# One ScalarE Silu in place of Tanh and a VectorE multiply, with the exponentials run in a row, in a fused attention and feed-forward kernel

## Chip, cores, metric

The kernel runs on one core of one Trainium2 chip. The metric is device time in microseconds; a kernel's figure is the median of its runs. All runs told here were of the fast state. Where two kernels are compared by a ratio, it is the mean time of one kernel's fast runs over that of the other's fast runs of the same rounds on the same chip, so it is not quite the ratio of the medians quoted beside it. In the traces PE is TensorE, PEld its weight loads, DVE is VectorE, ACT is ScalarE, POOL is GpSimd, and SPq is the DMA queue that SyncE feeds. "Idle" of an engine is time in which it runs nothing; an arrow names what ended that idle.

## The reference, cut

```python
def _attn_ref(q, k, v):                       # q, k, v: (8, 8, 576, 64), fp32
    q_s = np.exp(q - max_d); q_s = q_s / sum_d(q_s)      # softmax over the head dimension
    k_s = np.exp(k - max_s); k_s = k_s / sum_s(k_s)      # softmax over the sequence
    kv  = np.einsum('bhsd,bhse->bhde', k_s, v)
    return np.einsum('bhsd,bhde->bhse', q_s, kv)

def _moe_ref(x, w_in, w_out):                 # x: (4608, 512), d_ff = 2048
    h = x @ w_in
    g = h * (1.0 / (1.0 + np.exp(-h)))        # SiLU
    return g @ w_out
# output = _moe_ref(attention output, heads side by side)
```

So there are eight batches of attention, which need exponentials, and 4608 rows of a feed-forward layer, which need SiLU.

## The kernel before

The rows are worked in nine chunks of 512 (the first two have 576 and 448). The first product of a chunk, called mm1, has 16 blocks. Each fills one bank (a tile of 128 x 512 fp32 values in PSUM, `hps`), and ScalarE and VectorE empty it into `GT`. The banks come from a ring of five, which the attention's small products share.

```python
    PSB = {"ring": 5, "ops": 3}
    ...
    def mm1(t, fb):
        for off, size in part[t]:
            hps = ps.tile([128, TCH], FP32, name="hps", tag="ring", bufs=PSB["ring"])
            for c in range(NC):
                nc.tensor.matmul(out=hps[:, 0:size], lhsT=W1[...], rhs=XT[t][...], ...)
            sg = mp.tile([128, TCH], FP32, name="sg", bufs=3)
            nc.scalar.activation(out=sg[:, 0:size], in_=hps[:, 0:size], func=ACT.Tanh, scale=0.5)
            ...
                nc.vector.scalar_tensor_tensor(        # (tanh(h/2) + 1) * h = 2 SiLU(h)
                    out=GT[g][:, fb, col:col + n], in0=sg[:, h], scalar=1.0,
                    in1=hps[:, h], op0=ALU.add, op1=ALU.mult)
```

The factor of 2 is taken back by a scale of 0.5 where results are copied out. The second product is plain (`mm2`) for chunks 0 and 1. From chunk 2 on it is a Strassen scheme of seven half-size products, each in two parts, which needs sums and differences of GT blocks, made on VectorE (`presum`, tiles `SW`). A chunk's second product trails behind the mm1s of the next chunk.

Attention of batch `b` is woven into the list of these products, which the kernel calls units. `begin[b]` is the unit of chunk `b`'s first mm1, and a plan says how many units earlier each step is put into the program:

```python
    def exp(b, src, dst, cc):                          # 1152 columns of one half (cc) of q or k
        ...
        nc.scalar.activation(out=o, in_=jgd(st[b][src], cc), func=ACT.Exp)

    def plan_attn(b, u, sm, vs, tp, ks, ox, eng=nc.gpsimd):
        for cc in range(2):
            plan(u + sm[cc], lambda cc=cc: exp(b, "qt", "eq", cc))
            plan(u + sm[cc] + 1, lambda cc=cc: (qsum(b, cc), qnorm(b, cc, nc.gpsimd)))
        for cc in range(2):
            plan(u + sm[2 + cc], lambda cc=cc: exp(b, "kt", "ek", cc))
            plan(u + vs[cc], lambda cc=cc: vcast(b, cc, eng))
        plan(u + tp, lambda: tr_dma(b, nc.sync))       # qT: transposed by DMA
        ...                                            # loads of batch b + 1
        for cc in range(2):
            plan(u + ks[cc], lambda cc=cc: kv(b, cc))  # key-value products, two ring banks
            ...
        for cc in range(2):
            plan(u + ox[cc], lambda cc=cc: xt(b, cc))  # attention output -> XT, input of mm1
    ...
    for b in range(4, B):
        plan_attn(b, begin[b], (-38, -34, -30, -26), (-32, -28), -19, (-14, -10), (-7, -4))
```

`qsum` sums on VectorE, and `qnorm` multiplies and `vcast` casts on GpSimd. In the timelines below ScalarE and VectorE run their work in the order in which the program issues it (ScalarE at 151.52, 152.59 and 153.76 us, for one); so what is planned earlier also stands in front of what is planned later.

The softmax here doesn't subtract the row's maximum and nothing guards it: scores larger than these inputs give would overflow.

## Time and profile before

| | before |
|---|---|
| median of 4 runs | 283.75 us (282.66 to 283.88) |
| span of the profiled execution | 280.2 us |
| busy: TensorE / VectorE / ScalarE | 266.2 / 211.0 / 151.8 us |
| TensorE idle | 14.0 us |

These are the head and three lines of the groups from the page of the kernel before. Group lines read: line, engine, operation, tiles, size and count, then total busy us and mean ns of one, then idle of the engine before them and what ended it. PEclk is the granted TensorE clock in forty slices, in tenths.

```profile
span 280.2 us, 5788 instructions
PE 266.2 (95%) x2306; PEld 162.6 (58%) x2306; DVE 211.0 (75%) x393; ACT 151.8 (54%) x250; POOL 57.0 (20%) x44
PEclk9999999999999999999999999999999999999998
...
L214 ACT ACTIVATE sg<-hps 128x512 f32<-128x512 f32 (+3 forms) x160 | 87.5, 555 | 91.4 <-PE hps L206 68.4
L222 DVE SCALAR_TENSOR_TENSOR GT<-sg,hps 128x512 bf16<-128x512 f32 (+2 forms) x176 | 97.6, 582 | 44.3 <-ACT sg L214 43.7
L91 ACT ACTIVATE eq<-qt 128x1152 bf16<-128x1152 f32 x16 | 18.6, 1169 | 3.1 <-DMA qt<-in_q_dram 3.1
```

TensorE is the bound: 95% busy at full clock. The table of stretches shows where its 5% of idle is. The columns are the length, then busy us and count for each engine, then clock.

```profile
core 0: us, PE busy (x) PEld busy (x) DVE busy (x) ACT busy (x) POOL busy (x), PEclk, DMA share, GB/s
...
80.00:100.00 20.00, 18.84 (x166) 8.50 (x165) 16.56 (x32) 15.32 (x25) 5.92 (x5) 1.00 0.81 260
100.00:120.00 20.00, 20.00 (x210) 13.13 (x209) 17.97 (x33) 10.89 (x18) 4.36 (x3) 1.00 0.70 222
120.00:140.00 20.00, 20.00 (x145) 12.83 (x146) 17.82 (x26) 13.14 (x21) 7.36 (x4) 1.00 0.56 143
```

Next, ScalarE at the turn of a chunk: single exponentials stand between other work, and the one table load of the program is at its start.

```profile
0.73 1.28 ACT L366 ACT_TABLE_LOAD   x1 [0.73 <-PEq L534]
2.03 0.20 ACT L366 ACTIVATE dummy<-dummy 1x1 f32<-1x1 f32 x1
...
151.52 1.18 ACT L91 ACTIVATE eq<-qt 128x1152 bf16<-128x1152 f32 x1
152.59 1.28 ACT L214 ACTIVATE sg<-hps 128x512 f32<-128x512 f32 x2
153.76 1.15 ACT L91 ACTIVATE ek<-kt 128x1152 bf16<-128x1152 f32 x1
```

The load took 1.28 us and the next activation began 0.02 us after it. Tanh and Exp alternate without a load.

### The profile page before, as it was taken

What the parts mean: (1) busy time and instruction counts of PE and PEld (TensorE: products, weight loads), DVE (VectorE), ACT (ScalarE), POOL (GpSimd) and SP (SyncE); (2) the same over time, 40 slices, a digit from 0 to 9 for tenths busy, and PEclk for the clock granted to TensorE, in tenths of its full rate; (3) what the DMA queues carried; (4) which work ended last, traced back from release to release, by engine and by line L of the source; (5) the groups of instructions that cost most, each with busy time, mean ns of one, the idle gap of its engine ahead of it and who ended that gap; (6) DMA issues with size and microseconds to landing.
All of it is one profiled execution on the core that took longest, in us unless ns stands there. A gap on an engine that the chain in (4) does not pass through costs nothing.

```text
span 280.2 us, 5788 instructions
## 1 busy us (share of the span) xinstructions
PE 266.2 (95%) x2306; PEld 162.6 (58%) x2306; DVE 211.0 (75%) x393; ACT 151.8 (54%) x250; POOL 57.0 (20%) x44
## 2 busy tenths in 40 slices
PE   8689989988999999999999999999999999999992
PEld 3366654434444366666666666666666665666882
DVE  3975656896669898879987998799858585767721
ACT  5664663862785875476548654865265444544100
POOL 1551140063170370037003700370000000000000
PEclk9999999999999999999999999999999999999998
DMA  7999999988539949532982398235122013110244
GB/s 259 288 195 272 309 294 220 390 297 199 229 72 346 322 81 336 219 74 58 282 331 60 74 290 320 63 75 65 40 66 49 0 37 77 37 32 8 57 95 112
DMA packets 42378, 46.44 MB, mean 166 GB/s; under 512 B 18544, under 2 KB 29808, under 8 KB 42352
## 3 DMA queue, kind: packets, MB, share of 16 engines
q1 hardware_dynamic: 37312, 38.35, 46.7%
q0 software_dynamic: 5040, 7.73, 12.4%
q8 instruction: 18, 0.29, 0.4%
q14 instruction: 8, 0.07, 0.1%
HBM read 36.70 MB, written 9.44 MB: 165 GB/s over the span
## 4 chain that ended last, share of the span: by engine, by line
PE 75%; DMA 11%; DVE 9%; POOL 2%; issue 1%; ACT 1%; SPq 0%; ACTq 0%; DVEq 0%
PE hps L206 36%; PE ops L282 31%; DMA W<-in_moe_w_out_dram 8%; PE ops L340 5%; DVE GT L222 3%; DMA vt<-in_v_dram 3%; PE kvps L153 2%; DVE TW L258 2%; PE o L187 2%; DVE zq L105 1%; POOL W L381 1%; POOL W L387 1%; DVE oq L353 0%; SPq L82 0%; DVE kvn L166 0%
## 5 line engine op out<-in xcount | busy, mean ns | idle before, releaser
L206 PE MATMUL hps<-XT,W 128*128 128x512 bf16 (+3 forms) x640 | 143.1, 358 | 1.2 <-DVE GT L222 0.5
L214 ACT ACTIVATE sg<-hps 128x512 f32<-128x512 f32 (+3 forms) x160 | 87.5, 555 | 91.4 <-PE hps L206 68.4
L222 DVE SCALAR_TENSOR_TENSOR GT<-sg,hps 128x512 bf16<-128x512 f32 (+2 forms) x176 | 97.6, 582 | 44.3 <-ACT sg L214 43.7
L206 PEld LDWEIGHTS <-W 128*128 128x128 bf16 x640 | 61.2, 98 | 49.9 <-issue 3.5
L111 POOL TENSOR_TENSOR eq<-eq,rzq 128x1152 bf16<-128x1152 bf16 x14 | 30.4, 2174 | 117.9 <-DVE rzq L106 59.7
L282 PEld LDWEIGHTS <-GT 128*128 128x128 bf16 x448 | 43.5, 98 | 14.9 <-issue 1.0
L282 PEld LDWEIGHTS <-SW 128*128 128x128 bf16 x336 | 32.9, 98 | 11.1
L340 PE MATMUL ops<-W,GT 128*128 128x512 bf16 x128 | 33.1, 380 | 3.4 <-DVE GT L222 2.4
L282 PE MATMUL ops<-W,GT 128*128 128x256 bf16 x224 | 28.7, 273 | 0.0
L282 PE MATMUL ops<-TW,SW 128*128 128x256 bf16 x224 | 28.7, 273 | 0.0
L282 PE MATMUL ops<-TW,GT 128*128 128x256 bf16 x224 | 28.6, 273 | 0.0
L105 DVE TENSOR_REDUCE zq<-eq 128x18 f32<-128x1152 bf16 x16 | 21.6, 1348 | 6.4 <-ACT eq L91 6.4
L198 ACT CAST XT<-o 128x512 bf16<-128x512 f32 (+3 forms) x36 | 18.4, 564 | 6.8 <-PE o L187 6.8
L340 PEld LDWEIGHTS <-GT 128*128 128x128 bf16 x128 | 11.9, 98 | 15.8 <-DVE GT L222 3.6
L91 ACT ACTIVATE eq<-qt 128x1152 bf16<-128x1152 f32 x16 | 18.6, 1169 | 3.1 <-DMA qt<-in_q_dram 3.1
L91 ACT ACTIVATE ek<-kt 128x1152 bf16<-128x1152 f32 x16 | 18.5, 1157 | 1.6 <-DMA kt<-in_k_dram 1.6
L98 POOL CAST vaug<-vt 128x1152 bf16<-128x1152 f32 x12 | 17.7, 1503 | 0.0
L282 PE MATMUL ops<-W,SW 128*128 128x256 bf16 x112 | 14.2, 273 | 0.0
L240 DVE TENSOR_TENSOR SW<-GT 128x1024 bf16<-128x1024 bf16 x14 | 13.2, 943 | 0.3
L244 DVE TENSOR_TENSOR GT<-GT 128x1024 bf16<-128x1024 bf16 x14 | 13.4, 956 | 0.0
L299 DVE SCALAR_TENSOR_TENSOR u<-ops,s 128x512 f32<-128x512 f32 x14 | 9.6, 683 | 4.6 <-PE ops L282 4.6
L299 DVE SCALAR_TENSOR_TENSOR oq<-ops,u 128x512 f32<-128x512 f32 x14 | 9.6, 684 | 2.1 <-PE ops L282 2.1
(44 smaller groups left out, 125.8 us busy)
## 6 DMA issues: line engine op xcount, KB each, us to landing
qt<-in_q_dram SPq DMA_DIRECT2D x6, 1152.0 KB, 6.4
kt<-in_k_dram SPq DMA_DIRECT2D x6, 1152.0 KB, 8.8
vt<-in_v_dram SPq DMA_DIRECT2D x6, 1152.0 KB, 11.2
out_dram<-oq SPq DMA_DIRECT2D x42, 128.0 KB, 2.4
out_dram<-oq SPq DMA_DIRECT2D x60, 64.0 KB, 2.0
W<-in_moe_w_in_dram POOLq DMA_DIRECT2D x4, 512.0 KB, 9.7
W<-in_moe_w_out_dram POOLq DMA_DIRECT2D x4, 512.0 KB, 17.8
qt<-in_q_dram SPq DMA_DIRECT2D x2, 576.0 KB, 4.2
```

Source lines behind the costliest of these rows:

```text
L91: nc.scalar.activation(out=o, in_=jgd(st[b][src], cc), func=ACT.Exp)
L98: eng.tensor_copy(o, jgd(st[b]["vt"], cc))
L105: nc.vector.reduce_sum(out=st[b]["zq"][:, cc], in_=e, axis=AX.X)
L111: eng.tensor_tensor(out=e, in0=e, in1=r[:, :, :, None].to_broadcast([128, J, 2, D]), op=ALU.mult)
L198: nc.scalar.copy(out=x, in_=o1[g][:, 0:size])
L206: nc.tensor.matmul(out=hps[:, 0:size], lhsT=W1[:, c, fb * 128:(fb + 1) * 128], rhs=XT[t][:, c, off:off + size], start=(c == 0), stop=(c == ...
L214: nc.scalar.activation(out=sg[:, 0:size], in_=hps[:, 0:size], func=ACT.Tanh, scale=0.5)
L222: nc.vector.scalar_tensor_tensor(out=GT[g][:, fb, col:col + n], in0=sg[:, h], scalar=1.0, in1=hps[:, h], op0=ALU.add, op1=ALU.mult,)
L244: V.tensor_sub(quad(t, 0, f, 1), quad(t, 0, f, 0), quad(t, 0, f, 1))
L282: nc.tensor.matmul(out=o[:, a, :], lhsT=l(f), rhs=r(f), start=bool(first and a == 0 and f == 0), stop=(f == HF - 1), skip_group_check=True,)
L299: nc.vector.scalar_tensor_tensor(out=out, in0=o, scalar=0.5, in1=x, op0=ALU.mult, op1=ALU.add)
L340: nc.tensor.matmul(out=OP[t, tb], lhsT=GT[t][:, fc, tb * 128:(tb + 1) * 128], rhs=W2[:, fc, :], start=(fc == 0), stop=(fc == NFB - 1),)
```

## The change

The intent is to take 97.6 us of multiplies off VectorE by letting ScalarE write the finished SiLU. The built program shows the price: Silu and Exp need different tables, so ScalarE has to load a table at each change between them. To keep these few, exponentials are put in a row: two and two for batches 1 to 3, all four for batches 4 to 7. The program has 22 table loads in place of 1.

```diff
-            sg = mp.tile([128, TCH], FP32, name="sg", bufs=3)
-            nc.scalar.activation(out=sg[:, 0:size], in_=hps[:, 0:size], func=ACT.Tanh, scale=0.5)
...
-                nc.vector.scalar_tensor_tensor(
-                    out=GT[g][:, fb, col:col + n],
-                    in0=sg[:, h], scalar=1.0, in1=hps[:, h], op0=ALU.add, op1=ALU.mult,
-                )
+                nc.scalar.activation(out=GT[g][:, fb, col:col + n], in_=hps[:, h], func=ACT.Silu)
... (the five scales of 0.5 behind the second product become 1.0)
-        for cc in range(2):
-            plan(u + sm[cc], lambda cc=cc: exp(b, "qt", "eq", cc))
-            plan(u + sm[cc] + 1, lambda cc=cc: (qsum(b, cc), qnorm(b, cc, nc.gpsimd)))
+        for i, (x, y) in enumerate((("qt", "eq"), ("kt", "ek"))):
+            plan(u + sm[i], lambda x=x, y=y: [exp(b, x, y, cc) for cc in range(2)])
         for cc in range(2):
-            plan(u + sm[2 + cc], lambda cc=cc: exp(b, "kt", "ek", cc))
+            plan(u + sm[0] + 2 + 2 * cc, lambda cc=cc: (qsum(b, cc), qnorm(b, cc, nc.gpsimd)))
             plan(u + vs[cc], lambda cc=cc: vcast(b, cc, eng))
...
-    plan_attn(1, begin[1], (-18, -17, -11, -10), (-6, -5), -12, (-4, -3), (-2, 0), V)
-    plan_attn(2, begin[2], (-23, -21, -18, -15), (-14, -13), -15, (-10, -7), (-5, -3))
-    plan_attn(3, begin[3], (-26, -24, -20, -17), (-19, -16), -16, (-12, -9), (-6, -4))
+    plan_attn(1, begin[1], (-18, -11), (-6, -5), -11, (-4, -3), (-2, 0), V)
+    plan_attn(2, begin[2], (-21, -18), (-14, -13), -13, (-10, -7), (-5, -3))
+    plan_attn(3, begin[3], (-25, -20), (-19, -16), -16, (-12, -9), (-6, -4))
     for b in range(4, B):
-        plan_attn(b, begin[b], (-38, -34, -30, -26), (-32, -28), -19, (-14, -10), (-7, -4))
+        plan_attn(b, begin[b], (-34, -34), (-32, -28), -23, (-14, -10), (-7, -4))
```

More of the change, by code (lines that the diff above doesn't have):

```diff
@@ L221, in mm1 @@
                 h = slice(a - first, a - first + n)
-                nc.vector.scalar_tensor_tensor(
-                    out=GT[g][:, fb, col:col + n],
-                    in0=sg[:, h],
-                    scalar=1.0,
-                    in1=hps[:, h],
-                    op0=ALU.add,
-                    op1=ALU.mult,
-                )
+                nc.scalar.activation(out=GT[g][:, fb, col:col + n], in_=hps[:, h], func=ACT.Silu)
                 a += n
@@ L299, in add @@
             nc.vector.scalar_tensor_tensor(
-                out=out, in0=o, scalar=0.5, in1=x, op0=ALU.mult, op1=ALU.add
+                out=out, in0=o, scalar=1.0, in1=x, op0=ALU.mult, op1=ALU.add
             )
         if k == 1:
-            nc.scalar.activation(out=new("s1"), in_=o, func=ACT.Copy, scale=0.5)
+            nc.scalar.activation(out=new("s1"), in_=o, func=ACT.Copy, scale=1.0)
         elif k == 6:
@@ L311, in after @@
             if k == 2:
-                nc.scalar.activation(out=q, in_=o, func=ACT.Copy, scale=0.5)
+                nc.scalar.activation(out=q, in_=o, func=ACT.Copy, scale=1.0)
             else:
@@ L352, in store @@
         if dve:
-            nc.vector.tensor_scalar_mul(out=ost, in0=OP[t, tb], scalar1=0.5)
+            nc.vector.tensor_scalar_mul(out=ost, in0=OP[t, tb], scalar1=1.0)
         else:
-            nc.scalar.activation(out=ost, in_=OP[t, tb], func=ACT.Copy, scale=0.5)
+            nc.scalar.activation(out=ost, in_=OP[t, tb], func=ACT.Copy, scale=1.0)
         for i in range(2):
```

## The prediction

> **What bounds the kernel now.** TensorE. The page gives PE 266.2 of 280.2 us busy; in the stage table it is 20.00 of every 20 us from 100 to 260. It idles 14 us in all: about 4 before 20 us, 1.0 near 38 (a weight load), 3.8 between 40 and 100 (nearly all released by the VectorE multiply into GT), 5 at the end. VectorE (211 us) and ScalarE (152 us) are off the critical path after 100 us. So a free SiLU could gain only about 4 us.
>
> **Removed.** 176 VectorE multiplies, 97.6 us (678 ns for 512 columns): VectorE falls to about 113 us.
>
> **Added, on ScalarE.** Silu should cost what Tanh costs (597 ns; one can start every 0.49 us). The Trainium skill, "ScalarE: Activation LUTs", "The pipeline for one element", says all functions run at one element per cycle; no run here shows Silu yet. Silu and Exp do not share a table: the built program has 21 further table loads (4 each for batches 1 to 3, 2 each for 4 to 7, one at the start). The one in the trace takes 1283 ns, with 0.02 us until the next activation. The same page, "What ACT_TABLE_LOAD costs", gives about 2.66 us with a drain; I count 1.28. 21 x 1.28 = 27 us: ScalarE rises to about 180 us, still not full. The sum is not the cost.
>
> **Moved, on the critical path: the bursts.** Exponentials start every 1.07 us. Two with their switches block ScalarE for 4.8 us, four for 6.9, and no hps bank is emptied meanwhile. The ring has 5 banks; PE fills one in 0.87 us where mm1s come in a row. And the first Strassen product of a chunk needs the GT of that chunk's mm1 number 14, now queued behind the burst. Laid over the old timeline:
> - Batches 5 to 7: burst right after the XT copies. At 150 us: copies end 151.6, load 152.9, exponentials 157.3, load 158.6, Silu 159.2. PE wants that GT at 157.4: 1.85 us of stall each, 5.5 us.
> - Batch 4: mm1s without products between; five banks full at 98.9, freed at 102.7: 3.8 us, less 0.9 of old stalls: +2.9.
> - Batch 3: an XT copy behind a burst: 2.4 us, partly in place of old stalls: +1.5.
> - Batch 2: two bursts with one Silu between, 10 us; mm2 stalls 4.2 us against 2.4: +1.8.
> - Batch 1: two ring stalls of 0.8 to 0.9, partly hidden by the weight wait: +0.9.
>
> Sum +12.6 us.
>
> **Prediction.** 296.5 us (+4.5%), 8 in 10 between 289 and 304. Faster by over 2%: 0.02; within 2%: 0.10; slower by over 2%: 0.88.
>
> **What would show each step.** Table loads: 22 of about 1.28 us. Silu near 597 ns. DVE near 113 us, ACT near 180. PE busy hardly changed, but idle of 1.5 to 4 us at each burst, released by ScalarE's Silu (GT) or XT copy; none in the last two chunks, which have no exponentials. The chain of waits should pass through ACT there.
>
> **What would make it wrong.** Loads that cost a drain as well: each burst 2.8 us longer, some 20 us in all. Silu slower than Tanh. Bursts that fall where PE has slack, so that most stalls vanish: then within 2%. Long stalls could also lower the granted clock, which the PEclk slices would show. If late key loads hold up the exponentials, ScalarE would wait for DMA inside the burst.

## More of the kernel before

The kernel before took 281.7 to 286.0 us over all its runs, on several chips, so a difference of 1 us between calls means nothing by itself; waits read from traces are sharper.

From 100 us on nothing is left to gain on TensorE but the last few microseconds. The idle that VectorE's multiply makes lies before that, at three places. The timeline of TensorE shows the longest (idle before an instruction, and what ended it, stands in brackets):

```profile
64.27 0.39 PE L340 MATMUL ops<-W,GT 128*128 128x512 bf16 x1 [2.13 <-DVE GT L222]
```

After 20 us there are five idles of TensorE in that timeline: 0.96 (a weight load), 0.26, 2.13, 0.38 and 0.52 us, 4.25 us in all.

## The result, and the profile after

| | before | after |
|---|---|---|
| median | 283.75 us | 304.62 us (303.96 to 305.71, 4 runs) |
| ratio | 1 | 1.075, 95% interval 1.070 to 1.079 |
| span of the profiled execution | 280.2 us | 303.3 us |
| TensorE busy / idle | 266.2 / 14.0 us | 272.2 / 31.1 us |
| VectorE busy | 211.0 us | 121.0 us |
| ScalarE busy | 151.8 us | 178.7 us |

The page of the changed kernel, the lines that answer to those above:

```profile
span 303.3 us, 5523 instructions
PE 272.2 (90%) x2306; PEld 163.3 (54%) x2306; DVE 121.0 (40%) x217; ACT 178.7 (59%) x287; POOL 53.9 (18%) x44
PEclk9999999997999968999999999999999999999999
...
L220 ACT ACTIVATE GT<-hps 128x512 bf16<-128x512 f32 (+2 forms) x176 | 85.5, 526 | 86.9 <-PE hps L206 86.4
L220 ACT ACT_TABLE_LOAD x11 | 14.1, 1283 | 0.2
```

Silu of 512 columns took 602 ns (Tanh: 597), and each load 1283 ns. ScalarE is 59% busy, so it is not short of time in sum. TensorE lost 17.1 us to idle, and its busy time grew by 6.0 us at the same work. The timeline of TensorE names the idles; one of each kind for batches 5 to 7 is kept here:

```profile
36.05 1.14 PE L206 MATMUL hps<-XT,W 128*128 128x320 bf16 x8 [1.70 <-ACT GT L220]
43.00 1.14 PE L206 MATMUL hps<-XT,W 128*128 128x320 bf16 x8 [1.27 <-ACT GT L220]
67.68 0.39 PE L331 MATMUL ops<-W,GT 128*128 128x512 bf16 x1 [4.28 <-ACT GT L220]
83.27 2.21 PE L206 MATMUL hps<-XT,W 128*128 128x512 bf16 x8 [1.98 <-ACT GT L220]
90.73 1.89 PE L206 MATMUL hps<-XT,W 128*128 128x512 bf16 x8 [0.94 <-ACT GT L220]
110.06 3.57 PE L206 MATMUL hps<-XT,W 128*128 128x512 bf16 x8 [4.28 <-ACT GT L220]
145.36 0.28 PE L273 MATMUL ops<-W,GT 128*128 128x256 bf16 x1 [1.77 <-ACT GT L220]
149.57 0.61 PE L273 MATMUL ops<-TW,SW 128*128 128x256 bf16 x4 [0.90 <-DVE SW L233]
```

Eight matmuls of 512 columns took 1.89 us at 90.73 and 3.57 us at 110.06, right after the idle of 4.28 us. The timeline of ScalarE, GpSimd and VectorE around the burst of batch 5 shows what TensorE waited for at 145.36 and 149.57:

```profile
137.78 1.28 ACT L91 ACT_TABLE_LOAD   x1
139.07 2.22 ACT L91 ACTIVATE eq<-qt 128x1152 bf16<-128x1152 f32 x2
141.19 2.20 ACT L91 ACTIVATE ek<-kt 128x1152 bf16<-128x1152 f32 x2
143.41 1.28 ACT L220 ACT_TABLE_LOAD   x1
144.71 3.05 ACT L220 ACTIVATE GT<-hps 128x512 bf16<-128x512 f32 x6
145.29 2.12 POOL L111 TENSOR_TENSOR eq<-eq,rzq 128x1152 bf16<-128x1152 bf16 x1
145.82 2.13 DVE L231 TENSOR_TENSOR SW<-GT 128x1024 bf16<-128x1024 bf16 x1 [1.72 <-ACT GT L220]
147.99 1.52 DVE L233 TENSOR_TENSOR SW<-SW,GT 128x1024 bf16<-128x1024 bf16 x1
149.44 0.68 DVE L235 TENSOR_TENSOR GT<-GT 128x1024 bf16<-128x1024 bf16 x1
```

For 6.9 us, from 137.78 to 144.71, ScalarE empties no bank. The first Silu after it ends the 1.77 us idle. Then VectorE's two pre-additions, at 145.82 and 147.99, take 2.13 and 1.52 us; each takes 0.69 us in the median of its 14 instances. They end at 149.5, and that ends the idle of 0.90 us. GpSimd was multiplying when the first one started, and cast beside the second (147.35 to 148.97).

The table of stretches of the changed kernel around its two longest idles shows the clock:

```profile
66.00:68.00 2.00, 0.32 (x2) 0.21 (x3) 0.00 (x0) 1.99 (x4) 1.80 (x2) 1.00 0.63 122
68.00:70.00 2.00, 2.00 (x8) 0.75 (x7) 0.00 (x0) 1.04 (x3) 0.00 (x0) 0.55 1.16 197
...
110.00:112.00 2.00, 1.95 (x5) 0.69 (x5) 0.50 (x1) 2.00 (x6) 2.00 (x2) 0.50 0.00 0
112.00:114.00 2.00, 2.00 (x7) 0.88 (x6) 1.97 (x2) 0.89 (x2) 1.68 (x2) 0.50 0.35 69
```

After both idles of 4.28 us the granted clock was about half for some microseconds.

**The account.** The idles of TensorE after 20 us add up to 22.5 us (batch 1: 1.70 + 1.27; batch 2: 4.28; batch 3: 1.98 + 0.94; batch 4: 4.28; batches 5 to 7: 3 x (1.77 or 1.78, and 0.90)), against 4.25 us before. That is 18.2 us more. In the first 20 us, 0.9 us of idle has turned into busy time, and the idle at the end and in gaps too short to be listed is 0.2 us less, so that all idle is up by 17.1 us. Busy time is up by 6.0 us, those 0.9 us among them. Together that is the 23.1 us of the span.

### The profile page after: what moved, and what is told of

Same layout as the page of the kernel before. It is cut to its first block, busy times and chain, and to the rows that moved or that the text cites. A ratio compares the mean times of both kernels' runs of the same rounds, so it can differ in the third digit from the quotient of the medians.

```text
span 303.3 us, 5523 instructions
## 1 busy us (share of the span) xinstructions
PE 272.2 (90%) x2306; PEld 163.3 (54%) x2306; DVE 121.0 (40%) x217; ACT 178.7 (59%) x287; POOL 53.9 (18%) x44
## 4 chain that ended last, share of the span: by engine, by line
PE 60%; ACT 22%; DMA 8%; DVE 4%; issue 3%; POOL 1%; SPq 0%; ACTq 0%
PE hps L206 27%; PE ops L273 25%; DMA qt<-in_q_dram 6%; ACT ek L91 5%; ACT L220 4%; ACT L91 4%; ACT eq L91 4%; PE ops L331 4%; ACT GT L220 3%; DMA vt<-in_v_dram 3%; DVE SW L231 2%; PE kvps L153 2%; ACT XT L198 2%; PE o L187 2%; DVE SW L233 2%
## 5 line engine op out<-in xcount | busy, mean ns | idle before, releaser
L206 PE MATMUL hps<-XT,W 128*128 128x512 bf16 (+3 forms) x640 | 146.1, 363 | 10.8 <-ACT GT L220 10.2
L220 ACT ACTIVATE GT<-hps 128x512 bf16<-128x512 f32 (+2 forms) x176 | 85.5, 526 | 86.9 <-PE hps L206 86.4
L273 PE MATMUL ops<-W,GT 128*128 128x256 bf16 x224 | 30.1, 278 | 5.3 <-ACT GT L220 5.3
L231 DVE TENSOR_TENSOR SW<-GT 128x1024 bf16<-128x1024 bf16 x14 | 14.5, 1032 | 23.9 <-ACT GT L220 23.9
L91 ACT ACTIVATE eq<-qt 128x1152 bf16<-128x1152 f32 x16 | 17.8, 1156 | 2.7 <-DMA qt<-in_q_dram 2.6
L91 ACT ACTIVATE ek<-kt 128x1152 bf16<-128x1152 f32 x16 | 17.8, 1152 | 1.6 <-DMA kt<-in_k_dram 1.6
L98 POOL CAST vaug<-vt 128x1152 bf16<-128x1152 f32 x12 | 15.6, 1311 | 0.0
L220 ACT ACT_TABLE_LOAD x11 | 14.1, 1283 | 0.2
L233 DVE TENSOR_TENSOR SW<-SW,GT 128x1024 bf16<-128x1024 bf16 x14 | 13.0, 930 | 0.5
```

The source lines that it names most:

```text
L98: eng.tensor_copy(o, jgd(st[b]["vt"], cc))
L206: nc.tensor.matmul(out=hps[:, 0:size], lhsT=W1[:, c, fb * 128:(fb + 1) * 128], rhs=XT[t][:, c, off:off + size], start=(c == 0), stop=(c == ...
L220: nc.scalar.activation(out=GT[g][:, fb, col:col + n], in_=hps[:, h], func=ACT.Silu)
L231: V.tensor_add(S1[:, f], quad(t, 0, f, 1), quad(t, 1, f, 1))
L233: V.tensor_sub(S2[:, f], S1[:, f], quad(t, 0, f, 0))
L273: nc.tensor.matmul(out=o[:, a, :], lhsT=l(f), rhs=r(f), start=bool(first and a == 0 and f == 0), stop=(f == HF - 1), skip_group_check=True,)
```

## The experiments

**Theory.** What counts is not how much ScalarE does but what stands behind a burst. While it runs no bank is emptied, and TensorE stops where the ring runs out or a product needs a GT block queued behind the burst. The table loads lengthen each burst by 2.6 us, which is enough to pass the slack. Long idles also lower the clock, and GpSimd lengthens the pre-additions that the second product waits for. **Rivals.** (a) The loads cost their own time, so the loss goes with their number. (b) The moved order costs by itself, whatever the functions.

Medians in us; the ratio is to the kernel before in the same rounds (3 rounds each):

| run | what | median | before | ratio | table loads |
|---|---|---|---|---|---|
| e1_tanh | after, with Tanh for Silu (wrong result) | 280.92 | 282.16 | 0.995 | 1 |
| e2_bursts | arithmetic of before, plan of after | 308.51 | 282.16 | 1.092 | 1 |
| e3_warm | after, dummy matmuls in two idles | 301.19 | 282.16 | 1.067 | 22 |
| e4_pool_later | after, query sums and GpSimd work later | 313.23 | 282.16 | 1.110 | 22 |
| e5_mid | after, bursts of batches 4 to 7 mid-chunk | 295.43 | 282.11 | 1.047 | 22 |
| e6_spread | Silu, plan of before | 325.56 | 282.11 | 1.154 | 56 |
| e7_flips | after, 20 more loads in the last chunks | 310.84 | 282.11 | 1.101 | 42 |
| e8_casts_later | after, casts on GpSimd later | 301.47 | 282.11 | 1.070 | 22 |
| e9_flips_few | after, 8 more loads in the last chunks | 304.59 | 283.44 | 1.076 | 30 |
| e10_best | e5, batches 2, 3 replanned, multiplies moved | 291.18 | 283.44 | 1.029 | 22 |
| e11_b2 | after, batch 2 alone replanned | 301.26 | 283.44 | 1.063 | 22 |
| e12_queue | e10, transposing transfer earlier | 284.72 | 283.53 | 1.004 | 22 |

The 95% intervals are 0.3 to 0.9% to each side. All results but that of e1_tanh were correct.

### e1_tanh: no switch

```diff
-                nc.scalar.activation(out=GT[g][:, fb, col:col + n], in_=hps[:, h], func=ACT.Silu)
+                nc.scalar.activation(out=GT[g][:, fb, col:col + n], in_=hps[:, h], func=ACT.Tanh)
```

> The changed kernel with Tanh in place of Silu: the same instructions, sizes and order, but no table switch (wrong result on purpose). Theory (the switches inside the bursts make the stalls): table loads 22 -> 1, four exponentials block ScalarE for 4.3 us instead of 6.9; all stalls of TensorE at bursts vanish but about 1 us at batch 4; the granted clock stays full; 277 to 281 us, that is a little faster than the kernel before. Rival (the bursts and the moved order cost by themselves, or the third piece in chunk 0 does): it stays above 292 us.

Measured: 280.92 us, as the theory said. Of TensorE's idles after 20 us, 0.17 us (the weight load), two of 0.16 us, 1.44 us at batch 4 and three of about 0.3 us before the second product are left. The longest:

```profile
96.03 1.89 PE L206 MATMUL hps<-XT,W 128*128 128x512 bf16 x8 [1.44 <-ACT GT L220]
```

The clock did not drop after 20 us. The same instructions in the same order cost 24 us less (304.62 less 280.92, in different calls) when the two functions share a table. So the switches, where they stand, make the loss, and order, bursts and the third piece of chunk 0 do not. (A block of chunk 0 lies across two GT tiles, and the activation now writes GT itself, so it is cut into three pieces where Tanh took two: 176 activations in place of 160.)

### e2_bursts: the order alone, with the old arithmetic

The edit puts the Tanh, the VectorE multiply and the scales of 0.5 back into the changed kernel; the plan stays.

> The arithmetic of the kernel before (Tanh and VectorE multiply) with the exponentials and loads planned as in the changed kernel. Theory: bursts without switches are short enough for the ring: 281 to 286 us, within 1% of before; the VectorE stalls of before near batch 2 stay. Rival (order alone is the cost): 290 us or more. Against e1_tanh it also gives the worth of the removed multiplies: by theory 2 to 5 us.

Measured: 308.51 us; the expectation of 281 to 286 us was wrong by 22.5 us or more. The trace shows waits for the pre-additions, 2.55 us once and 4.4 us three times, and one of 2.46 us for a cast on GpSimd. VectorE's timeline in one of them:

```profile
135.85 0.69 DVE L222 SCALAR_TENSOR_TENSOR GT<-sg,hps 128x512 bf16<-128x512 f32 x1 [5.11 <-ACT sg L214]
136.46 1.35 DVE L105 TENSOR_REDUCE zq<-eq 128x18 f32<-128x1152 bf16 x1
...
139.23 1.34 DVE L105 TENSOR_REDUCE zq<-eq 128x18 f32<-128x1152 bf16 x1
...
140.79 1.27 DVE L240 TENSOR_TENSOR SW<-GT 128x1024 bf16<-128x1024 bf16 x1
...
142.58 2.00 DVE L242 TENSOR_TENSOR SW<-SW,GT 128x1024 bf16<-128x1024 bf16 x1
```

VectorE stood for 5.11 us, because its next multiply waited for a Tanh behind the burst. Then the held-up multiplies, the query sums and the pre-additions followed each other in its queue, until 144.6 us. The two pre-additions took 1.27 and 2.00 us in place of 0.69, with GpSimd at work beside them, which is 1.9 of the 4.4 us. So the order does cost by itself with the old arithmetic: rival (b) is right there, and it was not foreseen. Without the multiplies (e1_tanh) the same plan is 27.6 us faster. So the removed work is worth much in this order. In the old order it could save little: the idles that a multiply into GT ended there add up to 3.3 us (no run takes the multiplies away in the old order alone). That VectorE's queue is the cause is read from this trace; no run isolates it.

### e6_spread: Silu with the old order

The edit puts `plan_attn` and its numbers of the kernel before into the changed kernel.

> Silu with the exponentials planned one at a time as in the kernel before: 56 table loads instead of 22, ScalarE's busy time up by 44 us to about 222 us. Theory: each exponential now blocks ScalarE for 3.7 us, but in 12 us at the turn of a chunk there are four of them and two XT copies in 20 us of ScalarE work, so it lags by 7 us and TensorE stalls by 3 to 6 us in each batch from 2 to 7: 310 to 330 us, slower than the changed kernel. Rival (short blocks fit the ring, so spreading is better than a burst): under 304 us.

Measured: 325.56 us, as the theory said. The single waits are mostly 1 to 4 us; in batches 4 to 7 the largest is of 3 us for the `s` copy that ScalarE makes of a product. With Silu, collecting the exponentials, with the plan that goes with it, saves 21 us (325.56 less 304.62, in different calls). The two halves of the change belong together: each alone is worse than both.

### e3_warm: the clock

```diff
+    FILL = {(1, 9): 18, (3, 0): 18}
...
+            for _ in range(FILL.get((t, fb), 0)):
+                nc.tensor.matmul(out=hps, lhsT=warm[:, 0:128], rhs=warm, start=True, stop=True)
             for c in range(NC):
```

> The changed kernel with 18 dummy matmuls of 512 columns (3.9 us at full clock) put in front of one mm1 at each of the two 4.28 us stalls; they write a bank that the mm1 then overwrites, and fill time in which TensorE waits anyway. Theory (the two long idles drop the granted clock to half for about 3.5 and 6 us, which costs about 4.8 us): the clock stays at 1.0 there, the stalls shrink to under 1 us, and the time falls from 304.6 to 299 to 301 us. Rival (the lower clock is only a record, or costs nothing since ScalarE is behind anyway): 304 us or more.

Measured: 301.19 us, just above the 299 to 301 expected. The two idles of 4.28 us became 0.39 us each, and the clock there is 1.00, in the same stretches of the table:

```profile
68.00:70.00 2.00, 2.00 (x45) 0.97 (x43) 0.00 (x0) 1.10 (x3) 0.00 (x0) 1.00 1.23 203
...
110.00:112.00 2.00, 2.00 (x15) 1.27 (x14) 1.69 (x2) 1.72 (x4) 2.00 (x2) 1.00 0.00 0
```

The span fell from 303.3 to 299.1 us, 4.2 of the 4.8 us expected; the time fell by 3.4 us by medians and 0.8% by the ratios. Part was lost again: after the 1.98 us idle of batch 3 the clock fell to 0.50 for over 3 us in this run, and eight matmuls took 3.26 us there, against 2.21 us in the changed kernel after the same idle. In return the 0.94 us idle that followed is missing; it is missing in each run in which the clock dropped there. The dummy matmuls do no useful work; they only fill idle that was there.

### e4_pool_later and e8_casts_later: the pre-additions

In e4_pool_later the sums, multiplies and casts of batches 4 to 7 are moved later, and the transposing transfer five units later; the query and key loads keep their place.

```diff
-            plan(u + sm[0] + 2 + 2 * cc, ...qsum, qnorm...)
+            plan(u + sm[0] + (2 if b < 4 else 9) + (2 if b < 4 else 1) * cc, ...qsum, qnorm...)
...
-        plan_attn(b, begin[b], (-34, -34), (-32, -28), -23, (-14, -10), (-7, -4))
+        plan_attn(b, begin[b], (-34, -34), (-23, -22), -18, (-14, -10), (-7, -4))
```

> The changed kernel with the query sums, GpSimd's normalising multiplies and casts of batches 4 to 7 moved five to seven units later, and the loads left where they are. Theory (after a burst VectorE's two pre-additions, 0.69 us when alone, ran 2.1 and 1.5 us because GpSimd worked at the same time, and this made the 0.90 us waits of TensorE): they take about 0.7 us each, the three waits of 0.90 us vanish, 301 to 303 us. Rival (the chain Silu, addition, subtraction is too long behind a burst in any case): the waits stay and the time is unchanged within 0.5 us.

Measured: 313.23 us, slower. The pre-additions after a burst took 0.69 us each and the three waits of 0.90 us are gone, as the theory said. But the transposing transfer came too late: TensorE waited for qT 3.69 and 3.52 us, and the clock stood at about 0.5 for some 5 and 3 us of work after these two waits, which cost time too. As a test of time the run fails; it moved more than the suspected cause.

```diff
-        plan_attn(b, begin[b], (-34, -34), (-32, -28), -23, (-14, -10), (-7, -4))
+        plan_attn(b, begin[b], (-34, -34), (-24, -22), -23, (-14, -10), (-7, -4))
```

> The changed kernel with only GpSimd's casts of the values moved eight and four to six units later for batches 4 to 7; sums, multiplies and transposes stay, so nothing of the queries comes later. Theory (GpSimd at work beside VectorE's additions lengthens them and makes the three 0.90 us waits): the first addition is still partly beside GpSimd, the second alone at 0.69 us; the waits vanish or fall under 0.3 us and the time by 2 to 2.7 us, 302 to 302.7 us. Rival: the waits stay at 0.9 us.

Measured: 301.47 us; the three waits of 0.90 us are gone and no new ones came. The first pre-addition took 1.09 us; the second was expected at 0.69 us and took 1.52, beside a cast that had started at 145.33:

```profile
144.85 1.09 DVE L231 TENSOR_TENSOR SW<-GT 128x1024 bf16<-128x1024 bf16 x1 [1.72 <-ACT GT L220]
```

So the two runs show that GpSimd's place decides these waits. By medians the gain is 3.1 us and by ratios 0.5%, with intervals that overlap (1.065 to 1.075 against 1.070 to 1.079); the trace supports 2.7 us (3 x 0.90).

### e5_mid: the place of the bursts

```diff
-        plan_attn(b, begin[b], (-34, -34), (-32, -28), -23, (-14, -10), (-7, -4))
+        plan_attn(b, begin[b], (-24, -24), (-19, -18), -12, (-11, -8), (-5, -3))
```

> The changed kernel with the bursts of batches 4 to 7 moved from the end of a chunk into its first third, where TensorE alternates mm1 and products and fills one bank in 1.73 us; still two table loads for each of these batches, 22 in all. Theory (what counts is which bank or product waits behind a burst, not the loads): the stalls of 4.28 us and of 3 x (1.77 + 0.90) us and the clock drop after the first of them vanish, some 15 us: 288 to 292 us. Rival (the number of loads or ScalarE's busy time counts): 300 us or more.

Measured: 295.43 us, 9.2 us less than the changed kernel with the same 22 loads. All idles at the bursts of batches 4 to 7 are gone: 12.3 us of them, and the clock drop at batch 4. It missed 288 to 292 because the queries now came late: TensorE waited for qT 1.26, 1.61, 1.30 and 0.74 us, 4.9 us in all. The clock also dropped to 0.50 at batches 1 and 3, which this edit does not touch, after idles of 2.06 and 1.98 us.

### e7_flips and e9_flips_few: loads where TensorE has slack

```diff
+    def flip():
+        nc.scalar.activation(out=dummy, in_=dummy, func=ACT.Exp, scale=0.0)
+    for t in (NCH - 2, NCH - 1):
+        for i in (4, 6, 8, 10, 12):          # e9_flips_few: (4, 9)
+            plan(index[t * NFB + i], flip)
```

> The changed kernel with ten exponentials of one element put between mm1s in the last two chunks, where no other exponential is: 20 further table loads, 26 us more on ScalarE. Theory (a switch costs time only where an mm1, product or copy waits behind it; here TensorE takes 1.73 us for each bank): 304 to 306 us, no new idle of TensorE. Rival (each load costs its 1.28 us): 325 to 331 us.

Measured: 310.84 us, 6.2 us slower where none was expected. Two mm1s take 3.46 us, while two Silus and a flip take 2 x 0.49 + 2.76 = 3.74 us (an estimate from the 0.49 us between starts of activations and two loads with a tiny one; the trace has 3.91 us from one flip's load at 239.48 to the next at 243.39). ScalarE thus fell behind. The trace shows idles of 0.30 and 1.68 us late in the first of these chunks and 2.37 us at the end, after the last flips. These are 4.35 us. The rest of the 6.2 us is not traced to the flips: TensorE's busy time is up by 1.4 us in this profile, whose clock was below full from 66 to 74 us, far before the first flip, against 68 to 72 us in the changed kernel. So 26 us of loads cost some 4 to 6 us, not 0 and not 26.

> As e7_flips, but four instead of ten exponentials of one element in the last two chunks: 8 further table loads, 10.3 us more on ScalarE, at least four mm1s apart and none near a chunk's turn. Theory (the ten of e7_flips cost 6 us because ScalarE fell behind step by step until an XT copy and the last s copy came late; spread so that ScalarE catches up between them, switches are free): 304 to 305.5 us, no idle of TensorE in the last two chunks. Rival (each load costs a share, 6.2 us for 20 loads): about 307 us; (each its full time): 315 us.

Measured: 304.59 us against 304.62 for the changed kernel, with 8 more loads; ratio 1.0761 against 1.0748. TensorE has no idle in the last two chunks. Its table from 215 to 285 us:

```profile
215.00:240.00 25.00, 25.00 (x246) 15.93 (x245) 9.46 (x20) 12.94 (x22) 0.00 (x0) 1.00 0.18 43
240.00:265.00 25.00, 25.00 (x173) 15.94 (x171) 8.54 (x13) 16.05 (x27) 0.00 (x0) 1.00 0.18 43
265.00:285.00 20.00, 20.00 (x143) 13.73 (x141) 7.46 (x12) 12.57 (x19) 0.00 (x0) 1.00 0.12 27
```

Rival (a) falls: loads cost nothing where ScalarE can catch up before somebody waits.

### e11_b2: one batch

```diff
-    plan_attn(2, begin[2], (-21, -18), (-14, -13), -13, (-10, -7), (-5, -3))
+    plan_attn(2, begin[2], (-21, -17), (-14, -13), -13, (-7, -6), (-5, -3))
```

> The changed kernel with batch 2 alone replanned: the key burst one unit later, so that two Silus instead of one pass between its two bursts, and the key-value products three and one units later. Theory: the product that waited 4.28 us gets its GT in time; a ring stall of about 1.3 us takes its place; the idle is then too short for the clock to drop at batch 2: 299 to 301 us. Rival (ScalarE is short of time there whatever the order): 303 us or more, one stall of over 3 us or two of 2 us there.

Measured: 301.26 us, just outside the 299 to 301 expected and under the rival's 303. The idle of 4.28 us became one of 1.26 us. The clock dropped at batch 3 in this run, after its 1.98 us idle: eight matmuls took 2.92 us, and the 0.94 us idle behind it is missing.

### e10_best and e12_queue: how far Silu can go

e10_best takes e5_mid, the edit of e11_b2, and two more:

```diff
-    plan_attn(3, begin[3], (-25, -20), (-19, -16), -16, (-12, -9), (-6, -4))
+    plan_attn(3, begin[3], (-22, -15), (-19, -16), -15, (-8, -7), (-5, -3))
-        plan_attn(b, begin[b], (-34, -34), (-32, -28), -23, (-14, -10), (-7, -4))
+        plan_attn(b, begin[b], (-24, -24), (-21, -19), -14, (-11, -8), (-5, -3))
... qnorm(b, cc, nc.gpsimd if b < 4 else nc.vector)
```

> The best Silu version the runs point to: e5_mid, with the query multiplies of batches 4 to 7 on VectorE (so that the transposes come about 3 us earlier), batch 2's key burst one unit later behind one more Silu and its key-value products later, and batch 3's bursts off the XT copies. Still 22 table loads. Theory: e5_mid less 4.2 us of waits for qT, less 3 us and a clock drop of 1.7 us at batch 2, less 1 to 2 us at batch 3: 284 to 287 us, so all but 1 to 2% of the loss comes from where the bursts stand. Rival: 292 us or more. It is not expected to beat the kernel before, whose whole idle that this change can touch was 4 us.

Measured: 291.18 us, above the 284 to 287 expected and just under the rival's 292. Batch 2 improved as expected, but the waits for qT stayed at 1.27, 1.63 and 1.33 us, with a fourth of 0.77 us, although the queries were ready earlier. The DMA queue's timeline of e10_best shows why: VectorE's multiply ended at 116.2 us.

```profile
116.46 2.38 SPq L320 DMA_DIRECT2D out_dram<-oq  x4
118.96 2.77 SPq L122 DMA_TRANSPOSE qT<-eq  x1
```

Four stores of a product stand ahead of the transfer in the same in-order queue. The last run puts the transfer ahead of them:

```diff
-        plan_attn(b, begin[b], (-24, -24), (-21, -19), -14, (-11, -8), (-5, -3))
+        plan_attn(b, begin[b], (-24, -24), (-21, -19), -18, (-11, -8), (-5, -3))
```

> e10_best with one number changed: the transposing transfer of batches 4 to 7 is issued four units earlier, ahead of the stores of a chunk's first finished product on the same in-order queue. In e10_best the VectorE multiply ended at 116.2 us, but the transfer was issued at 119.0, behind four stores that waited for a product. Theory: it is issued some 2.5 us earlier, qT lands before TensorE asks for it, and the three waits of 1.27, 1.63 and 1.33 us vanish: 286.5 to 288 us. Rival (the transfers are slow for another reason, such as the input loads beside them): the waits stay over 1 us and the time at 291 us.

Measured: 284.72 us against 283.53 for the kernel before, ratio 1.004 with an interval of 0.996 to 1.013, so the same. The queue's timeline of e12_queue shows the transfer first:

```profile
115.22 2.71 SPq L122 DMA_TRANSPOSE qT<-eq  x1
...
119.78 2.81 SPq L320 DMA_DIRECT2D out_dram<-oq  x4
```

The transfers landed a median of 4.6 us after issue (6.3 in e10_best) and no wait for qT is left. It gained more than the 286.5 to 288 us expected: against e10_best the span is 6.8 us shorter, of which 3.8 us is idle and 3.0 us TensorE's busy time. The four waits for qT alone were 5.0 us. At least 1.7 us of the busy time is clock, and not the work of the edit, which leaves batch 1 alone: e10_best had a slice at 0.7 after a 2.23 us idle at batch 1, and e12_queue, with 1.67 us there under the same plan, had none. The page of e12_queue:

```profile
span 282.4 us, 5515 instructions
PE 265.8 (94%) x2306; PEld 162.3 (57%) x2306; DVE 122.0 (43%) x225; ACT 177.5 (63%) x287; POOL 35.6 (13%) x36
```

ScalarE carries the same 22 loads and 26 us more than before, VectorE 89 us less, and the kernel is as fast as before. Neither it nor e1_tanh beats the kernel before clearly. A version without switches and with a right result was not tried.

## Why the prediction was right or wrong

- **Bound, and the most that can be gained: right.** e1_tanh, with the multiplies gone and no switches, is 0.5% faster than before (ratio 0.991 to 1.000, so the same within the noise).
- **Removed work: right in kind.** VectorE fell by 90 us (98 predicted); the difference is not slower other work: the durations of all other VectorE instructions add up to 129 us before and 128 us after. Neighbours overlap in the trace (a multiply that starts at 88.45 lasts 0.68 us, and the next instruction starts at 89.05), so the 97.6 us of one group contain time that its neighbours cover as well, and the busy time falls by less.
- **Silu's cost, number and cost of loads: right.** 602 ns against 597, 22 loads of 1283 ns, ScalarE 178.7 us against 180. The prediction set aside the 2.66 us with a drain that the Trainium skill, "ScalarE: Activation LUTs", "What ACT_TABLE_LOAD costs", gives. The trace agrees with its 1283 ns for the load and shows no drain: one switch took 1.29 us from load to next start (137.78 to 139.07), and the load after the exponentials began 0.02 us after the last of them (143.39 to 143.41). That page's statement, in "Step-by-step: what each stage is for", that every function takes the same time per element agrees with the 602 and 597 ns.
- **Mechanism, stalls behind bursts: right, and closely sized at batches 2, 5, 6 and 7.** Predicted 4.2 us at batch 2 and 1.85 us at 5 to 7, measured 4.28 and 1.77 to 1.78; batch 4, 3.8 against 4.28. e1_tanh, e5_mid and e11_b2 confirm it.
- **Time: wrong.** 304.6 us lies above the range of 289 to 304, and the loss of 20.9 us is 1.6 times the predicted 12.7. The step that failed is "Sum +12.6 us":
  - *The clock was left out of the sum.* The prediction expected "PE busy hardly changed" and named a lower clock only under "What would make it wrong", although two of its own stalls were near 4 us. TensorE's busy time rose by 6.0 us, of which about 5 is half clock after the two 4.28 us idles (an estimate: 0.9 of the 6.0 lies in the first 20 us; and stretches of 2 us at 0.55, 0.60 and three times 0.50 lack 4.7 us of full clock). e3_warm took 4.2 us of it off the span.
  - *A wait was missed.* The second product of batches 5 to 7 waits 0.90 us for pre-additions lengthened beside GpSimd: 2.7 us, shown by e4_pool_later and e8_casts_later.
  - *Two stalls were too small.* Batch 1 cost 2.97 us instead of 1.7, and batch 3 had a second stall of 0.94 us.
  - *Old stalls were credited too high.* 0.9 us of old idle was taken off twice, at batch 3 and at batch 4. In all 5.0 us was taken off, and the trace before has 4.25. The terms missed here (some 5, 2.7, 1.3 + 0.5 and 0.75 us) and 0.5 us more at batch 4 make up the gap between 12.6 us and the 23.1 us of the profiled span.
- **The rest.** No idle in the last two chunks: right. ScalarE waiting for DMA in a burst: did not happen on any scale.

## What to carry to other kernels

When a function needs another table, do not count the loads; ask who stands behind the longest stretch in which that engine serves nobody, and how many buffers the bound engine has until then. With the same 22 loads this kernel took 305 us or 285 us, by the place of the bursts and of the work that follows them, of one DMA in its queue, and by 8 multiplies moved from GpSimd to VectorE. When stalls of the bound engine come out near 4 us, put the clock that they cost into the sum, and look what else starts in the same moment beside the engine that has to catch up.

## What the Trainium skill lacked or had wrong

- "ScalarE: Activation LUTs", "What ACT_TABLE_LOAD costs", gives about 2.66 us for every switch, load and drain. In these runs a switch cost 1283 ns, as the page has it for the load alone, and 0.02 us on either side of it; the drain was not there.
- No page says with which functions Silu shares a table. The 22 loads of this program, against one when Tanh stands in its place (e1_tanh), show that Exp is not among them.
- "TensorE: Matmul & The Clock Gate", "What's actually happening", gives the drop to half clock after at least one idle window of about 3.4 us. After 4.28 us the clock was 0.50 to 0.55, which agrees. But after only 1.98 us it also fell to 0.50 in e3_warm (for over 3 us), e5_mid and e11_b2, though not in the changed kernel after the same idle (2.21 us for eight matmuls, no lower clock in the records), and after 2.06 us in e5_mid and 2.23 us in e10_best, though not after 2.21 us in e11_b2. Shorter idles can cost clock too; what decides it is not shown.
- "SBUF — State Buffer", "Who interferes with whom", says that a VectorE instruction with two SBUF inputs contends with a GpSimd instruction that reads SBUF. The runs agree: the pre-addition took 0.69 us alone and 2.13 us beside GpSimd's multiply. The page has no duration for such an addition beside GpSimd; here it was three times as long, and three waits of 0.90 us came of it.
